# Attention scores as eight tiles of 32 rows by 64 keys, each over only the queries that its keys can meet

## The chip, the cores and the metric

The kernel runs on one core of a Trainium2 chip. The metric is device time in microseconds (us), the median of several executions.

## The reference, cut to what matters

Two independent problems of the same shape, A and B: 2048 positions, model width 1024, 32 heads of 32, and a sliding window of 256 keys.

```python
qkv = (x @ wqkv)                       # split into q, k, v; 32 heads, Dh = 32
scores = einsum("bhqd,bhkd->bhqk", q, k) * (Dh ** -0.5)
mask = (q_idx - k_idx >= 0) & (q_idx - k_idx < 256)
p = softmax(where(mask, scores, -1e9))
out = einsum("bhqk,bhkd->bhqd", p, v) @ wo
```

A block of 128 keys j thus meets the queries of blocks j (the lower triangle), j+1 (all) and j+2 (the upper triangle).

## The kernel before

Four heads form a group g. Its (key block, query block) pairs are handled in 180 *sessions* of four slots of 128 queries. Consecutive pairs with the same key block are one *run*; the sessions are mostly of runs of 3+1, 2+2 or 1+3 slots. A session issues the score matmuls, ScalarE takes the exponential of the whole buffer, GpSimd zeroes what the mask excludes, and some sessions later PV matmuls (p times v) use the result. In between, TensorE works on the projections.

```python
    def session(now):
        es = entries_of(now)
        n = len(es)
        st = ps_st.tile([P, 4, SLOTS, P], F32, name="st")     # four PSUM banks, one for each head
        ...
        while a < n:                                          # for each run a..b
            ...
            for r in range(4):                                # four heads = four 32-row tiles
                nc.tensor.matmul(
                    st[:, r, a:b, :],
                    lhsT=kT[32 * r:32 * r + 32, j * P:(j + 1) * P],
                    rhs=qT[32 * r:32 * r + 32, q * P:(q + b - a) * P],
                    start=True, stop=True, tile_position=(32 * r, 0))
            a = b
        pt = ptp.tile([P, 4, SLOTS, P], BF16, name="pt")
        nc.scalar.activation(out=pt[...], in_=st[...], func=ACT.Exp, bias=-SHIFT, scale=cfg.scale)
        # ... GpSimd masks of the first and third block of a run
```

Around PV, which uses four tiles of 128 rows by 32 columns, the projections are cut in the same way to avoid a change of array shape; ahead of a score session, where the shape does change, a median of 105 ns lies between the end of the streaming and the first score matmul. That takes four pairs of weight load and matmul where one would do:

```python
    def by_columns(out, lo, hi, lhsT, rhs, start, stop):
        if whole[0]:
            nc.tensor.matmul(out[:, lo:hi], lhsT=lhsT, rhs=rhs, ...)
            return
        for c in range(0, P, 32):
            nc.tensor.matmul(out[c:c + 32, lo:hi], lhsT=lhsT[:, c:c + 32], rhs=rhs, ...,
                             tile_position=(0, c))
```

## Time and profile before

| | before |
|---|---|
| time, median (lowest to highest) | 609.3 us (609.28 to 609.43, 3 runs) |
| span of the profiled execution | 607.6 us |
| TensorE on the chain that ended last | 96% |
| score matmuls (line L451), their share of the chain | 1488, 10% |
| TensorE instructions in the profile (matmuls and weight loads) | 25,624 |

In the profile, PE is TensorE's matmuls and PEld its weight loads. A group's line gives shapes and count, then busy time and mean duration, then the idle time before it and what ended that. A timeline line gives start, length, engine, source line, what is written and read, and in brackets the idle time before. A matmul's recorded length is not the time that it adds (one of 512 columns is recorded with 379 ns, and the next group of the same shape starts 216 ns after it), so the distance between starts says more than lengths do.

### The profile page before, as it was taken

The numbers are of one execution on the slowest core, as the hardware profiler recorded it, in microseconds if no ns is written. First come the engines' busy times: TensorE is split into PE (matmuls) and PEld (weight loads), VectorE is DVE, ScalarE is ACT, GpSimd is POOL, SyncE is SP. The second block draws the span as 40 slices with busy tenths as digits, with TensorE's granted clock in tenths as the row PEclk, the third lists the DMA queues.
The fourth block names the chain that finished last, engine by engine and source line by source line (L and its number), as shares of the span: only waits on it lengthen the run. The fifth ranks groups of instructions, "written<-read, shape, count | busy, mean of one in ns | idle before, by whom it ended". The sixth has DMA issues, their size and how long they took to land.

```text
span 607.6 us, 28768 instructions
## 1 busy us (share of the span) xinstructions
PE 593.6 (98%) x12786; PEld 344.3 (57%) x12838; DVE 468.4 (77%) x1199; ACT 441.1 (73%) x376; POOL 326.3 (54%) x630
## 2 busy tenths in 40 slices
PE   8999999999999999999999999999999999999996
PEld 6555466656655756564556756655455665545443
DVE  1677889898898898897888887898888887897200
ACT  3778887788888887877778877777776777785332
POOL 0565666665666666556555565555555655554000
PEclk9999999999999999999999999999999999999999
DMA  9833110111015501442111100112021040113222
GB/s 234 182 92 89 37 38 3 38 38 39 3 38 90 114 14 30 82 101 77 38 37 38 38 4 8 33 37 81 2 68 34 4 106 21 55 58 120 72 79 64
DMA packets 86802, 35.47 MB, mean 58 GB/s; under 512 B 65552, under 2 KB 86160, under 8 KB 86672
## 3 DMA queue, kind: packets, MB, share of 16 engines
q1 hardware_dynamic: 85632, 33.31, 22.2%
q8 instruction: 102, 1.67, 1.2%
q10 hardware_dynamic: 1040, 0.26, 0.2%
q14 instruction: 28, 0.23, 0.1%
HBM read 17.83 MB, written 8.39 MB: 43 GB/s over the span
## 4 chain that ended last, share of the span: by engine, by line
PE 96%; ACT 2%; issue 1%; DMA 1%; ACTq 0%
PE pp L176 44%; PE pp L172 28%; PE acc L513 13%; PE st L451 10%; ACT pt L459 1%; DMA oT<-in_A_x_dram 1%; PE acc L582 0%; PE pp L568 0%; ACT kT L190 0%; ACT vt L190 0%; PE st L582 0%; ACT osb L190 0%; PE pp L805 0%; ACTq L190 0%
## 5 line engine op out<-in xcount | busy, mean ns | idle before, releaser
L459 ACT ACTIVATE pt<-st 128x2048 bf16<-128x2048 f32 x180 | 338.0, 1878 | 91.6 <-PE st L451 73.5
L471 POOL TENSOR_SCALAR_AFFINE_SELECT pt<-pt 128x512 bf16<-128x512 bf16 x224 | 154.5, 690 | 145.7 <-ACT pt L459 143.1
L467 POOL TENSOR_SCALAR_AFFINE_SELECT pt<-pt 128x512 bf16<-128x512 bf16 x256 | 179.2, 701 | 85.8 <-ACT pt L459 85.8
L524 DVE RECIPROCAL rinv<-acc 128x128 f32<-128x128 f32 x128 | 122.0, 953 | 57.0 <-PE acc L513 56.4
L176 PE MATMUL pp<-xT,wqk 128*32 128x512 bf16 x2712 | 163.1, 379 | 0.0
L481 DVE TENSOR_TENSOR both<-pt 128x512 bf16<-128x512 bf16 x224 | 137.1, 651 | 0.0
L176 PEld LDWEIGHTS <-wqk 128*32 128x32 bf16 x2712 | 69.3, 97 | 54.2 <-issue 0.4
L172 PE MATMUL pp<-xT,wqk 128*128 128x512 bf16 (+1 forms) x323 | 76.7, 369 | 4.1 <-issue 2.4
L176 PE MATMUL pp<-wv,xT 128*32 128x256 bf16 x2436 | 75.9, 273 | 0.0
L451 PE MATMUL st<-qT,kT 32*128 32x384 bf16 (+2 forms) x1488 | 71.5, 269 | 0.1
L176 PEld LDWEIGHTS <-xT 128*32 128x32 bf16 x2436 | 63.8, 97 | 6.2
L529 DVE STREAM_SHUFFLE wide<-rinv 128x128 f32<-128x128 f32 x256 | 64.6, 298 | 0.0
L513 PE MATMUL acc<-pt,vt 128*32 128x128 bf16 (+1 forms) x2160 | 63.3, 239 | 0.0
L172 PE MATMUL pp<-wo_sb,oT 128*128 128x512 bf16 (+1 forms) x269 | 59.3, 373 | 1.3 <-issue 0.9
L451 PEld LDWEIGHTS <-kT 32*128 32x128 bf16 x1488 | 22.2, 92 | 64.5 <-issue 63.3
L190 ACT CAST osb<-pp 128x512 bf16<-128x512 f32 (+1 forms) x52 | 30.0, 577 | 39.1 <-PE pp L172 24.4
L531 DVE TENSOR_TENSOR oT<-acc,wide 128x256 bf16<-128x256 f32 x128 | 54.3, 425 | 4.4
L176 PE MATMUL pp<-wo_sb,oT 128*32 128x512 bf16 x952 | 55.6, 379 | 0.0
L172 PEld LDWEIGHTS <-wqk 128*128 128x128 bf16 x362 | 33.4, 98 | 37.0 <-issue 6.8
L172 PE MATMUL pp<-wv,xT 128*128 128x256 bf16 x415 | 50.9, 273 | 1.4 <-ACT kT L190 0.6
L513 PEld LDWEIGHTS <-vt 128*32 128x32 bf16 x2160 | 35.9, 96 | 26.4 <-issue 24.1
L172 PEld LDWEIGHTS <-xT 128*128 128x128 bf16 x415 | 38.9, 98 | 12.0 <-issue 6.1
(46 smaller groups left out, 386.5 us busy)
## 6 DMA issues: line engine op xcount, KB each, us to landing
out_dram<-osb SPq DMA_DIRECT2D x63, 128.0 KB, 1.8
wqk<-in_B_wqkv_dram SPq DMA_DIRECT2D x32, 128.0 KB, 2.5
wqk<-in_A_wqkv_dram SPq DMA_DIRECT2D x24, 128.0 KB, 2.7
wo_sb<-in_A_wo_dram SPq DMA_DIRECT2D x16, 128.0 KB, 2.2
wv<-in_B_wqkv_dram SPq DMA_DIRECT2D x16, 128.0 KB, 2.8
wo_sb<-in_B_wo_dram SPq DMA_DIRECT2D x16, 128.0 KB, 2.4
oT<-in_A_x_dram SPq DMA_DIRECT2D x4, 256.0 KB, 5.4
wv<-in_A_wqkv_dram SPq DMA_DIRECT2D x2, 512.0 KB, 5.9
```

What stands on the lines that cost most here:

```text
L172: nc.tensor.matmul(out[:, lo:hi], lhsT=lhsT, rhs=rhs, start=start, stop=stop, skip_group_check=True)
L176: nc.tensor.matmul(out[c:c + 32, lo:hi], lhsT=lhsT[:, c:c + 32], rhs=rhs, start=start, stop=stop, tile_position=(0, c), skip_group_check=True)
L190: nc.scalar.copy(out=out, in_=in_)
L451: nc.tensor.matmul(st[:, r, a:b, :], lhsT=kT[32 * r:32 * r + 32, j * P:(j + 1) * P], rhs=qT[32 * r:32 * r + 32, q * P:(q + b - a) * P], st ...
L459: nc.scalar.activation(out=pt[:, :, :n, :].rearrange("p r a q -> p r (a q)"), in_=st[:, :, :n, :].rearrange("p r a q -> p r (a q)"), func= ...
L467: nc.gpsimd.affine_select(out=blk, in_=blk, pattern=[[0, 4], [1, P]], compare_op=ALU.is_ge, fill=0.0, base=0, channel_multiplier=-1)
L471: nc.gpsimd.affine_select(out=blk, in_=blk, pattern=[[0, 4], [-1, P]], compare_op=ALU.is_gt, fill=0.0, base=0, channel_multiplier=1)
L481: nc.vector.tensor_tensor(out=both[:, :, h, :], in0=pts[s0][:, :, a0, :], in1=pts[s1][:, :, a1, :], op=ALU.add)
L513: nc.tensor.matmul(acc[32 * r:32 * r + 32, o:o + w_], lhsT=lhsT, rhs=src[:, r, :, :], start=(x == 0), stop=(x == len(moves) - 1), tile_pos ...
L524: nc.vector.reciprocal(out=rinv[:], in_=acc[:, 2 * P:3 * P])
L529: nc.vector.stream_shuffle(out=wide[:, h * P:(h + 1) * P], in_=rinv[:], mask=[16 * h] * 32)
L531: nc.vector.tensor_tensor(out=oTs[(pi, k)][:, t, (p % 2) * 256:(p % 2 + 1) * 256], in0=acc[:, 0:256], in1=wide[:], op=ALU.mult)
```

## The change

The intent: at either end of a run, a corner of 64 keys by 64 queries is always masked, so it need not be computed. The lower 64 keys of a block meet only the first 320 of a run's 384 queries, the upper 64 only the last 320. With tiles of 32 rows by 64 keys, each half streams only those. The buffer is kept for the whole program and zeroed once, so that the places no longer written hold finite numbers.

```diff
+HALF = 64
...
-        st = ps_st.tile([P, 4, SLOTS, P], F32, name="st")
+        st = scores
+        flat = st[:].rearrange("p r a q -> p r (a q)")
...
-            for r in range(4):
-                nc.tensor.matmul(
-                    st[:, r, a:b, :],
-                    lhsT=kT[32 * r:32 * r + 32, j * P:(j + 1) * P],
-                    rhs=qT[32 * r:32 * r + 32, q * P:(q + b - a) * P],
-                    start=True, stop=True, tile_position=(32 * r, 0))
+            for c in range(2):
+                lo = HALF if c == 1 and q == j else 0
+                hi = (b - a) * P - (HALF if c == 0 and q + b - a == j + 3 else 0)
+                keys = slice(j * P + c * HALF, j * P + (c + 1) * HALF)
+                for r in range(4):
+                    rows = slice(32 * r, 32 * r + 32)
+                    nc.tensor.matmul(
+                        flat[c * HALF:(c + 1) * HALF, r, a * P + lo:a * P + hi],
+                        lhsT=kT[rows, keys], rhs=qT[rows, q * P + lo:q * P + hi],
+                        start=True, stop=True, tile_position=(32 * r, c * HALF),
+                        skip_group_check=True)
             a = b
...
+    scores = ps_st.tile([P, 4, SLOTS, P], F32, name="st")
+    nc.vector.memset(scores[:, 1:4], 0.0)
...
-    flips.append(ps_st.tile([P, 4, SLOTS, P], F32, name="st")[:, 0].rearrange("p a q -> p (a q)"))
+    flips.append(scores[:, 0].rearrange("p a q -> p (a q)"))
...
+    nc.vector.memset(scores[:, 0:1], 0.0)
```

## The prediction

> **What bounds the kernel now.** I read the busy shares first, then the chain that ended last, then the groups by line and form, then the timeline around one score session, and last the start times of single matmuls in the trace. From the page:
>
> ```profile
> PE 593.6 (98%) x12786; PEld 344.3 (57%) x12838; DVE 468.4 (77%) x1199; ACT 441.1 (73%) x376; POOL 326.3 (54%) x630
> ...
> PE 96%; ACT 2%; issue 1%; DMA 1%; ACTq 0%
> PE pp L176 44%; PE pp L172 28%; PE acc L513 13%; PE st L451 10%; ACT pt L459 1%; DMA oT<-in_A_x_dram 1%; PE acc L582 0%; PE pp L568 0%; ACT kT L190 0%; ACT vt L190 0%; PE st L582 0%; ACT osb L190 0%; PE pp L805 0%; ACTq L190 0%
> ```
>
> TensorE is the chain for 96% of the span, and the score matmuls of L451 are 10% of it, some 61 us. The other engines have slack of 23% and more. The groups split by form:
>
> ```profile
> L451 PE MATMUL st<-qT,kT 32*128 32x384 bf16 x448 | 37.7, 326 | 0.1
> L451 PE MATMUL st<-qT,kT 32*128 32x128 bf16 x544 | 29.6, 219 | 0.0
> L451 PE MATMUL st<-qT,kT 32*128 32x256 bf16 x496 | 25.6, 273 | 0.0
> ```
>
> Four matmuls (one for each head, each in its own 32 rows) make a group: 112 groups of 384 columns, 136 of 128 and 124 of 256. The busy times can't be added up, because the durations overlap; the timeline is the better view of what a session of four slots costs:
>
> ```profile
> 302.36 0.60 PE L176 MATMUL pp<-xT,wqk 128*32 128x512 bf16 x8
> ...
> 302.89 0.12 PEld L451 LDWEIGHTS <-kT 32*128 32x128 bf16 x8 [0.42 <-issue]
> 302.90 0.40 PE L451 MATMUL st<-qT,kT 32*128 32x384 bf16 x8
> 303.22 0.29 PEld L513 LDWEIGHTS <-vt 128*32 128x32 bf16 x16 [0.21 <-issue]
> 303.23 0.51 PE L513 MATMUL acc<-pt,vt 128*32 128x128 bf16 x16
> 303.40 1.88 ACT L459 ACTIVATE pt<-st 128x2048 bf16<-128x2048 f32 x1 [0.75 <-ACT vt L190]
> ```
>
> The first row is two groups of four; within one array shape the trace starts the next group 216 ns after one of 512 columns, 109 ns after one of 256, 56 ns after one of 128: 0.418 ns a column plus 2.5 ns. So this projection has streamed its columns at 302.36 + 2x0.216 = 302.79 us. The scores start 0.11 us later although no operand is missing, and the PV matmuls start 0.33 us after the scores. Of that 0.33 the streaming of 384 + 128 columns is only 0.214.
>
> Taking the start times of all 180 sessions, the medians are 105 ns from the end of the streaming before to the first score matmul, and 328 ns from there to the next other matmul. In the session above the 384-column group took 174 ns up to the next group's start (160 streaming, 2.5 usual, some 11.5 more that only a first group after a change of shape shows), and the 128-column group 153 ns up to the first PV matmul (53 streaming, 100 for the change back). A session thus costs about 433 ns, 180 of them 78 us, and **only half of it, 213 ns, is columns streaming**. The rest is two changes of array shape.
>
> Is PE waiting for the exponential, which must have read the score buffer (there is just one)? The waits say the opposite:
>
> ```profile
> ACT pt L459 <- PE st L451: 73.5, 113, 1.3
> PEld L451 <- issue: 63.3, 177, 0.4
> ```
>
> ScalarE waits for the scores 113 times, and what precedes the score weight loads is "issue", not ScalarE. So time taken off or put on a score session goes straight to the end.
>
> [...] a 128-column load is read as four runs of 32 and takes 90 to 98 ns, no longer than a 32-column one (92 to 97). A 64-column load can then be the longest of the three; no run here shows it yet. [...] The trace shows tiles overlapping in one direction only at a time: four row tiles in the scores, and four column tiles in the PV and projection matmuls, start within 9 to 11 ns of each other. Rows and columns together occur nowhere in it.
>
> **The change part by part.**
>
> *Removed: columns.* A full run of three query blocks goes from 384 columns to 320 in each half of the keys: the lower 64 keys meet queries 0 to 319, the upper 64 meet 64 to 383. With 4 slots a session there are three main patterns, 56 sessions each, and 12 others. If the two halves truly overlap and each goes ahead independently:
> - runs 3+1: lower 320+128 = 448 columns, upper 320+64 = 384. The longer is 448 instead of 512.
> - runs 2+2: lower 192+256, upper 256+192: 448.
> - runs 1+3: lower 64+320, upper 128+320: 448.
> Eight of the other twelve keep 512, four go to 448. So 172 sessions lose 64 columns: 172 x 64 x 0.417 ns = **4.6 us**, the ceiling. It is under 1%.
>
> *Added: issue skew.* Score matmuls go from 1488 to 2976, weight loads likewise. The trace issues a pair of load and matmul each 3.4 ns or so. The upper half's four come after the lower half's four, so they start about 14 ns later. In the 2+2 and 1+3 patterns the upper half ends last, so all 14 ns lie at the end of the session; in 3+1 the lower half ends last, and the skew is hidden. Playing the order of issue through for all 180 sessions with these numbers leaves a gain of 27 ns for 3+1, 13 for the next two, mean 17: **3.1 us** in all.
>
> *Added: slower weight loads.* The 11.5 ns that a first group shows is about what 32 columns take (13 ns), so I read it as the exposed weight load. If a 64-column load is unsplit, 64 columns stand there instead: +13.5 ns a session, 180 x 13.5 = 2.4 us. Then **0.6 us** of gain remain. Later loads of the session are issued ahead while the first group streams and stay hidden. I take a point between 0.6 and 3.1, 2.0 us.
>
> *Unchanged:* both edges of 100 to 105 ns (the tiles are still not those of the neighbours), the exponential (still 128x2048, 1878 ns), the masks, PV, and the order in which everything is emitted, since the scheduler's constants are not touched.
>
> *The fills.* The buffer becomes permanent and is zeroed once, so that places never written hold finite numbers; the masks still remove them. A 256-column fill takes 0.27 us on VectorE in the trace, so the 1536-column fill is an estimated 1.6 us, and stands in 4.73 us of idle time before VectorE's first copy. The 512-column one is an estimated 0.55 us in the 1.30 us idle before its next work at 11.93 us, and the first scores only start at 13.83 us. Both cost nothing. I see no new wait from keeping the buffer: the first score matmul already waits for the previous exponential.
>
> Sum: 609.3 - 2.0 = **607.3 us**.
>
> **The rivals.**
> 1. *The two halves serialise.* If the tiles of one 32-row strip with different columns don't overlap, a session streams about 896 columns instead of 512: 384 x 0.417 = 160 ns more, 180 times, 28.8 us, 638 us. For it: no instruction of the kernel combines row and column tiles, and both halves write the same four PSUM banks. Against: PV's four column tiles write one bank and have different moving data, and still start within 10 ns[...]. I give it 10%.
> 2. *The halves overlap but advance in lockstep*, each group waiting for the longer of both. Then 2+2 keeps 256+256 = 512 and gains nothing but pays the skew; two thirds of the saving are left, minus the costs above: about 607.5 to 610. For it: in the trace all tiles of a group have the same number of columns. [...]
> 3. *The score buffer or ScalarE becomes the bound.* ScalarE is busy 73% and gets its scores no later than now; ends at the same time, 607 to 609.
> 4. *The edges change,* [...] Each 10 ns on one edge is 180 x 10 = 1.8 us either way. The trace shows such an effect already: the edge is 96 ns after 128x128 matmuls, 106 after four column tiles, which is the skew of the four.
>
> **Range and chances.** Over 2% faster would need 12.2 us, nearly three times the ceiling of streaming; only shorter edges could give it: 0.03. Over 2% slower needs 68 ns a session, so serialisation or something like it: 0.11. Within 2%: 0.86. For the range I take the ceiling and some edge gain below, 603.5, and edges or loads 10 to 20 ns worse than assumed above, 611.
>
> **What would show it.** The score line has 2976 matmuls with at most 320 columns. Right: eight start within about 28 ns, the 320-column group starts its successor some 147 to 161 ns after itself instead of 174, and the score session goes from 328 ns to 311 to 325, with the edge before it still at 105. The first-group excess reads 11 or 25 ns and settles the weight load. Wrong: the upper half starts only when the lower half has streamed (rival 1), or a 2+2 session stays at 328 or more (rival 2), or PE now shows waits on ScalarE. The prediction fails if PE's other lines change their spacing, for instance through the larger number of instructions.

## The result, and the profile after

| | before | after |
|---|---|---|
| time, median (lowest to highest), 6 runs each | 609.37 us (609.18 to 610.27) | 610.9 us (610.07 to 612.45) |
| ratio | | 1.0026 (95%: 1.0008 to 1.0043) |
| span of the profiled execution | 607.6 us | 608.4 us |
| score matmuls | 1488 | 2976 |

A ratio is the mean time of one kernel's runs over that of the other's of the same rounds, so it is not quite the ratio of the medians. Executions over 1.5% slower than the fastest of the same kernel are left out of the means. The change makes the kernel a little slower, by a quarter of a per cent.

From the page of the changed kernel, busy shares and the chain that ended last:

```profile
PE 593.7 (98%) x14274; PEld 351.9 (58%) x14326; DVE 470.7 (77%) x1201; ACT 441.1 (73%) x376; POOL 326.2 (54%) x630
...
PE 96%; ACT 2%; issue 1%; DVE 0%; ACTq 0%
PE pp L177 44%; PE pp L173 28%; PE acc L520 14%; PE st L458 10%; ACT pt L466 1%; PE pp L577 1%; PE acc L591 0%; ACT kT L191 0%; ACT vt L191 0%; PE st L591 0%; ACT osb L191 0%; DVE top L126 0%; PE pp L815 0%; DVE ones L791 0%; ACTq L191 0%
```

At this resolution nothing has moved: the scores (now L458) are still 10% of the chain. By form the columns are trimmed as intended, and the weight loads got slower, 103 ns where those of before had 92 (first line: before; the others: after):

```profile
L451 PEld LDWEIGHTS <-kT 32*128 32x128 bf16 x1488 | 22.2, 92 | 64.5 <-issue 63.3 <-DVE top L184 0.8 <-ACT kT L190 0.4
```

```profile
L458 PE MATMUL st<-qT,kT 32*64 32x320 bf16 x896 | 38.6, 307 | 0.3
L458 PE MATMUL st<-qT,kT 32*64 32x128 bf16 x560 | 30.3, 226 | 0.0
L458 PEld LDWEIGHTS <-kT 32*64 32x64 bf16 x2976 | 29.1, 103 | 65.0 <-issue 64.0 <-DVE top L185 0.8
```

**Where the time went.** I compared the two traces from each score session's start to the next. For each pattern of session the median difference is taken as the session's own (for the twelve rare sessions, the difference in the sessions themselves); what an interval has above that is something else. Between the two traces of before this account leaves 0.02 us, so it can be trusted to a few hundredths. This gives, in the profiled executions:

| | us |
|---|---|
| first score session starts (loads at the start) | -0.46 |
| the 180 sessions themselves | -1.00 |
| five intervals in which TensorE stood still | +1.51 |
| nine intervals with some 44 ns more each | +0.40 |
| the rest, up to the start of the last session | -0.04 |
| after the start of the last session | +0.35 |
| sum: span 607.62 to 608.37 | +0.76 |

The profiled execution is a fast one of the changed kernel (610.1 us, median 610.9), so the table accounts for about half of the 1.5 us between the medians. The first row is scatter (the second execution of the changed kernel had +0.70). The sessions did save 1.0 us: 3+1 sessions, from the first score matmul to the next other weight load, went from 325 to 312 ns, 2+2 and 1+3 stayed (326), and the edge ahead of all of them became 2 ns shorter. The two rows that took more than that away are shown next.

**The stops.** This is the timeline of the weight loads near one of them in the changed kernel:

```profile
209.21 0.11 PEld L177 LDWEIGHTS <-xT 128*32 128x32 bf16 x4
209.53 0.14 PEld L458 LDWEIGHTS <-kT 32*64 32x64 bf16 x11 [0.21 <-issue]
210.00 0.11 PEld L458 LDWEIGHTS <-kT 32*64 32x64 bf16 x5 [0.33 <-issue]
210.26 0.22 PEld L173 LDWEIGHTS <-xT 128*128 128x128 bf16 x3
```

and the same session in the kernel before:

```profile
209.78 0.12 PEld L451 LDWEIGHTS <-kT 32*128 32x128 bf16 x8 [0.21 <-issue]
210.11 0.99 PEld L172 LDWEIGHTS <-xT 128*128 128x128 bf16 x10 [0.21 <-issue]
```

In the middle of sixteen like loads, all from the same finished kT, nothing starts for 0.41 us, and the profile gives the reason as "issue": no semaphore event, from which it infers who released whom, and no other engine. The matmuls stop with them: one session's, with the gap in the changed kernel (0.80 us) and without it in the one before (0.40 us):

```profile
209.53 0.80 PE L458 MATMUL st<-qT,kT 32*64 32x64 bf16 x16
```

```profile
209.78 0.40 PE L451 MATMUL st<-qT,kT 32*128 32x128 bf16 x8
```

Seven such gaps over 120 ns are in this trace (28.56, 78.67, 210.00, 249.14, 344.63, 381.60 and 486.33 us; that at 249 shows no excess in the account above, that at 345 some 0.05 us, the other five are its five intervals). Counting TensorE's instructions in program order, its sequencer's included, **all seven stand at the same place modulo 256**. I call each stretch of 256 TensorE instructions from one such place to the next a block, and the place its edge. The trace has a queue q8 of the kind "instruction", with packets of 16,384 bytes. Their number is about one for each 256 of TensorE's instructions (102 packets for 25,624 matmuls and weight loads before, 100.1 times 256; 114 for 28,600 after, 111.7 times 256), so I take them for TensorE's (first before, then after; packets, MB, share):

```profile
q8 instruction: 102, 1.67, 1.2%
```

```profile
q8 instruction: 114, 1.87, 1.3%
```

Each of the seven gaps ended 1.24 to 1.59 us after the last such packet had landed. My reading, from these traces alone: a packet brings a block's instructions, and at these places TensorE gets to the next block before it can be used. Two things in the traces fit that. Pairing packets and block edges in order, a packet starts a median of 0.5 us after the edge before in the changed kernel; for the stop at 210.00 us it started 0.81 us after that edge, took 1.00 to land, and TensorE went on 1.45 later, 3.26 us in all, where the block's own instructions needed 2.84. And of 1,333 edges in the twelve traces of this text none was passed sooner than 1.09 us after the landing of its packet; in the two traces of before none sooner than 1.67.

**The waits on ScalarE.** The kernel before, around one session:

```profile
397.11 0.40 PE L451 MATMUL st<-qT,kT 32*128 32x384 bf16 x8
...
397.60 1.88 ACT L459 ACTIVATE pt<-st 128x2048 bf16<-128x2048 f32 x1 [1.20 <-PE st L451]
...
399.38 0.58 ACT L190 CAST qT<-pp 128x512 bf16<-128x512 f32 x1
...
400.01 0.10 PEld L176 LDWEIGHTS <-wqk 128*32 128x32 bf16 x3 [0.19 <-issue]
```

and the changed kernel:

```profile
397.11 0.38 PE L458 MATMUL st<-qT,kT 32*64 32x320 bf16 x16
...
397.64 1.88 ACT L466 ACTIVATE pt<-st 128x2048 bf16<-128x2048 f32 x1 [1.23 <-PE st L458]
...
399.42 0.58 ACT L191 CAST qT<-pp 128x512 bf16<-128x512 f32 x1
...
400.05 0.10 PEld L177 LDWEIGHTS <-wqk 128*32 128x32 bf16 x3 [0.23 <-issue]
```

The scores start at the same time and TensorE gets through them sooner, yet the exponential starts 0.04 us later, so the copy behind it on ScalarE is 0.04 us later, and TensorE, which needs the projection bank that this copy frees, too. In all 3+1 sessions the exponential now starts a median of 529 ns after the first score matmul instead of 498, in 2+2 470 instead of 449, in 1+3 449 as before. (The profile has the semaphore of the last score matmul of a 3+1 session at a median of 457 ns after the first one's start instead of 426.) Only a few sessions have no slack for it. Seven of the nine intervals end at a projection matmul that waits for a copy of ScalarE, an eighth at one that waits for a copy of VectorE. The ninth, at 344.6 us, is no such wait: it is the gap at the block edge at 344.63.

**The fills** cost nothing, as their lines in the groups by form and VectorE's idle time around them show (1.34 and 0.49 us; the first scores at 13.37 us):

```profile
L572 DVE MEMSET st<- 128x1536 f32 x1 | 1.3, 1338 | 0.3 <-issue 0.3
L609 DVE MEMSET st<- 128x512 f32 x1 | 0.5, 485 | 0.1
```

### The profile page after: what moved, and what is told of

Read it like the earlier page. It is cut to its first block, busy times and chain, and to the rows that moved or that the text cites. A ratio compares the mean times of both kernels' runs of the same rounds, so it can differ in the third digit from the quotient of the medians.

```text
span 608.4 us, 31747 instructions
## 1 busy us (share of the span) xinstructions
PE 593.7 (98%) x14274; PEld 351.9 (58%) x14326; DVE 470.7 (77%) x1201; ACT 441.1 (73%) x376; POOL 326.2 (54%) x630
## 4 chain that ended last, share of the span: by engine, by line
PE 96%; ACT 2%; issue 1%; DVE 0%; ACTq 0%
PE pp L177 44%; PE pp L173 28%; PE acc L520 14%; PE st L458 10%; ACT pt L466 1%; PE pp L577 1%; PE acc L591 0%; ACT kT L191 0%; ACT vt L191 0%; PE st L591 0%; ACT osb L191 0%; DVE top L126 0%; PE pp L815 0%; DVE ones L791 0%; ACTq L191 0%
## 5 line engine op out<-in xcount | busy, mean ns | idle before, releaser
L458 PE MATMUL st<-qT,kT 32*64 32x320 bf16 (+4 forms) x2976 | 71.3, 259 | 0.3
L458 PEld LDWEIGHTS <-kT 32*64 32x64 bf16 x2976 | 29.1, 103 | 65.0 <-issue 64.0
```

Of the source, the lines that this page charges most:

```text
L458: nc.tensor.matmul(flat[c * HALF:(c + 1) * HALF, r, a * P + lo:a * P + hi], lhsT=kT[rows, keys], rhs=qT[rows, q * P + lo:q * P + hi], star ...
```

## The experiments

The theory to be tested, called F in the expectations: the trimming saves a little, and the added instructions make TensorE run out of instructions at the edges of blocks of 256, which costs more. The first expectations speak of 0.6 us saved and 1.45 us of stops; that was from a rougher account, which had put part of the stops into the sessions, and the table above (1.00 and 1.51) replaces it. All outputs of all runs were correct. The counts of gaps below are of gaps over 120 ns at a block's edge with a packet landing 1.05 to 1.7 us before their end; a few tenths of a microsecond in each sum would be there without a stop (a change of array shape, 103 to 105 ns ahead of a score session, may fall in one).

### The changed kernel once more

No edit.

> The changed kernel once more, for its spread and for a second trace. Theory F (starved front end): the score sessions save 0.6 us, but five times TensorE stood still for 0.14 to 0.41 us with no wait on anything, each time where its instruction stream enters another block of 256, and these 1.45 us together are the loss. Then this trace again shows a few such stops, all at the same place of a block, not necessarily in the same blocks, and the time is 609.8 to 612.5 us, more scattered than before's. Rival S (start and end): the loss is the new fills or the end of the program; then the trace shows a later first score session or a later end, and no stops. Rival N (noise): ratio to before within 0.1% of 1.

Measured: 611.33 us (610.89 to 612.37), 1.0027 (1.0014 to 1.004) of the kernel before. The trace has five gaps at block edges, 2.2 us in all, at 29.93, 111.09, 211.99, 251.18 and 383.76 us. Three of these are the instructions at which the first trace stopped at 28.56, 210.00 and 381.60 us, now for 587, 850 and 347 ns instead of 375, 411 and 124. By the same account as above its sessions save 1.00 us, the stops cost 2.11 and the waits on copies (eight) 0.35. At one of the three the stop is longer where the packet came later: for 411 ns at 210.00 us the packet started 0.81 us after the edge before, for 850 ns at 211.99 us 1.23 us after. That this makes the kernel's larger scatter fits, but isn't shown. The start lay 0.70 us late here and 0.46 early in the first trace: rival S gets no support.

### The kernel before once more

No edit.

> The kernel before once more, for a second trace. Theory F (the front end starves where 256 TensorE instructions run in less than about 3.2 us): no stop of 60 ns or more that the first trace of before lacks, since its fastest block took 3.2 us there and got by; the first score session within 0.7 us of the first trace's, which is the scatter of the loads at the start. Rival: stops come by chance with any kernel; then this trace has some too.

Measured: 609.4 us. Against the first trace of before no interval between sessions differs by more than 25 ns, and neither of the two traces has a gap at a block edge.

### As many instructions, but the old tiles

```diff
 # on the kernel before
-            for r in range(4):
-                nc.tensor.matmul(st[:, r, a:b, :], lhsT=kT[...], rhs=qT[32*r:32*r+32, q*P:(q+b-a)*P], ...)
+            w = (b - a) * P // PARTS                  # PARTS = 2
+            for c in range(PARTS):
+                for r in range(4):
+                    nc.tensor.matmul(flat[:, r, a*P + c*w:a*P + (c+1)*w], lhsT=kT[...],
+                                     rhs=qT[32*r:32*r+32, q*P + c*w:q*P + (c+1)*w], ...)
```

> The kernel before, with each score matmul of four row tiles cut into two halves of its queries: as many TensorE instructions as the changed kernel, but neither 64-key tiles nor fewer columns, nor a kept buffer. Theory F: the score sessions alone give +5 ns each (2.5 ns for each further group), +0.9 us; beyond that the stops appear here too, at block edges, for 0.5 to 3 us more: 610.8 to 613 us. Rival T (the 32 by 64 tiles cause the stops): no stops, 610.2 to 610.5 us.

Measured: 612.74 us (612.08 to 614.67), ratio 1.0057 (1.0043 to 1.0071). Sessions went from 325 to 330 ns, +0.91 us in all as expected. The trace has five gaps at block edges, 1.7 us. One of them, at the same place in the program as the one shown above:

```profile
210.85 0.14 PEld L454 LDWEIGHTS <-kT 32*128 32x128 bf16 x11 [0.21 <-issue]
211.39 0.11 PEld L454 LDWEIGHTS <-kT 32*128 32x128 bf16 x5 [0.39 <-issue]
```

Eleven loads, a stop, five loads, exactly as with the 64-key tiles. So the stops need neither the new tiles nor the trimmed columns nor the kept buffer; **the number of instructions brings them**. Rival T falls. The intervals of 44 ns did not come here. They do not belong to the 64-key tiles, though: the next run has six of 40 ns with the old tiles. What they follow is how late the exponential of a 3+1 session starts, 498 ns after the first score matmul in the kernel before, 511 here, 529 in the changed kernel, 584 in the next run.

### Three times as many added

```diff
-PARTS = 2
+PARTS = 4
```

> The kernel before with each score matmul cut into four quarters of its queries: 4464 score matmuls more than before, three times what the change adds, same array shape. Sessions +15 ns each by the 2.5 ns for every further group, +2.8 us. Theory F: blocks of 256 go by still faster, so stops get more and longer, at least twice the 1.6 us of the cut in two: 615 us or more. Rival (the stops have to do with tiles of 64 columns or with chance): 612 to 613 us.

Measured: 632.64 us (631.47 to 634.34), ratio 1.0386 (1.037 to 1.0402). 36 gaps at block edges, 14.9 us. The view of waits now has whole lines for TensorE waiting for nothing but its own issue, where the kernel before, once the first microseconds are over, has only "PE pp L172" with 3.5 us in 22 pieces, none longer than 0.2:

```profile
PE pp L177 <- issue: 2.8, 5, 1.3
PE st L454 <- issue: 2.1, 4, 0.8
PE acc L516 <- issue: 0.8, 2, 0.4
```

The columns are total us, times, longest us. The direction was expected, the size not: three times the added instructions gave nearly nine times the stops. Part of the time is not stops: 2+2 sessions took 341 ns as worked out, but 3+1 and 1+3 sessions took 369 and 378, by their medians some 56 x (28 + 37) ns = 3.6 us more than expected. These have pieces of 32 columns, and the trace shows where the time is: groups of four such matmuls start 25 ns apart, where 32 columns and the usual 2.5 ns would be 16. Nine ns at each of three or four groups are the 28 and 37. Why they come no closer isn't shown.

### What the trimmed columns are worth

```diff
 # on the changed kernel
-                lo = HALF if c == 1 and q == j else 0
-                hi = (b - a) * P - (HALF if c == 0 and q + b - a == j + 3 else 0)
+                lo = 0
+                hi = (b - a) * P
```

> The changed kernel with all columns kept: eight tiles of 32 by 64, each over all queries of the run. What the fewer columns are worth: by the spacing in the trace 26 to 31 ns a session, so a session of some 352 ns instead of 325 and +5.5 us over the changed kernel less what the stops change: 614 to 617 us. A rival in which column tiles share the read of their queries or in which the halves advance in lockstep would leave 2+2 sessions as long as in the changed kernel (326 ns).

Measured: 616.59 us (615.07 to 616.91), ratio 1.0105. Sessions of every main pattern take 352 or 353 ns: 27 ns more than the 2+2 and 1+3 sessions of the changed kernel, 40 more than its 3+1 sessions. So the trimmed columns are worth what streaming says, 64 x 0.417 = 27 ns, and splitting a session into 64-key tiles without trimming costs 27 (353 against 325 or 326 before). The two nearly cancel.

### The order of the halves

```diff
+        cols = [...]                      # columns of each half in this session
+        upper = cols[1] > cols[0]
...
-            for c in range(2):
+            for c in ((1, 0) if upper and a == 0 else (0, 1)):
```

> The changed kernel with the upper half first in the first run of the sessions in which the upper half is the longer chain (the 1+3 pattern). If the 14 ns of issue skew at the end of a session are real, the 1+3 sessions go from 326 to 313 ns, 56 x 13 = 0.7 us less than the changed kernel, with the stops unchanged in kind: 609 to 611.5 us. If the skew is no cost, sessions stay at 326.

Measured: 610.95 us (610.33 to 612.44), ratio 1.0022. The 1+3 sessions fell from 326 to 312 or 313 ns, as expected, so the issue skew is real and is avoidable there. Over all sessions the saving against before rose from 1.00 to 1.73 us, the 0.7 us expected. The kernel's time did not follow clearly (0.4 us under the changed kernel of the same rounds, with overlapping ranges): this trace has six gaps at block edges, 2.7 us. An inconclusive run for the total, a clear one for the session.

### Sixteen tiles of 32 by 32

```diff
-HALF = 64
+HALF = 32
...
-            for c in range(2):
-                lo = HALF if c == 1 and q == j else 0
-                hi = (b - a) * P - (HALF if c == 0 and q + b - a == j + 3 else 0)
+            for c in range(4):
+                lo = c * HALF if q == j else 0
+                hi = (b - a) * P - ((3 - c) * HALF if q + b - a == j + 3 else 0)
```

> Sixteen tiles of 32 rows by 32 keys, each over the queries that its 32 keys can meet (288 columns of a full run instead of 320). Theory on the weight load: the excess of the first group falls from 24.5 ns (64 columns) back to about 11.5 (32 columns)[...]; the skew grows to 40 ns, 12 pairs of 3.4. Together the sessions come to some 313 ns, 2.3 us less than before. Theory F then loses all of that and more to the stops, since it adds 8928 instructions: 611 to 616 us. If the excess stays at 24.5 ns, the reason isn't the number of columns loaded.

Measured: 631.8 us (628.71 to 633.49), ratio 1.0372; 36 gaps at block edges, 16.5 us. What a first group takes above its streaming until its tiles start the second group is 12.7 ns in the kernel before (loads of 128 columns), 26.7 in the changed one (64), and 13.3 here (32). It goes with the runs of columns that the trace records as a load's source: four runs of 32 for each of the 1488 score loads before, one run of 64 for each of the 2976 in the changed kernel. My reading, an estimate from the 0.417 ns a column of the same traces, is that one run stands exposed once a session: 13.3 ns for 32 columns, 26.7 for 64. It isn't shown that what is exposed is the load. Up to the next weight load the sessions took 286, 326 and 326 ns, a mean of 313 as worked out. But what counts is the next matmul, and in 3+1 sessions it comes 32 ns after its weight load here, where 2 ns are usual. Up to the next matmul they took 318, 329 and 328 ns, where the kernel before has 327, 329 and 327 and the one with the better order 314, 330 and 314. So of the 2.3 us expected of the sessions only some 0.4 came, and **the sixteen tiles' sessions are not the best ones**. Why that matmul comes late isn't shown.

### Only where it gains

The new tiles only in sessions in which the longer half has fewer columns than before and the halves differ; the four old matmuls in the others.

```diff
 # on the kernel with the better order
+            if cols[0] == cols[1] or max(cols) == SLOTS * P:
+                for r in range(4):
+                    ...                        # the old matmul of 128 keys, into the kept buffer
+                a = b
+                continue
```

> Candidate: 64-key tiles only in the sessions that gain by them (3+1, and 1+3 with the upper half first in the first run), the four old 128-key matmuls in the 2+2 sessions and the others that gain nothing. Sessions save 1.5 us against before; 944 score matmuls are added instead of 1488, so fewer stops, though most of the fast blocks still have some added: 0.5 to 1.5 us of stops. 608.3 to 609.8 us, within 0.2% of before either way, and 1 to 2.5 us under the changed kernel.

Measured: 609.57 us (608.87 to 610.41), ratio 0.9997 (0.9983 to 1.001): the same as before. Sessions saved 1.76 us. Fewer stops came, three, but one took 1.46 us:

```profile
487.66 0.38 PE L470 MATMUL st<-qT,kT 32*64 32x128 bf16 x15
489.20 0.29 PE L470 MATMUL st<-qT,kT 32*64 32x320 bf16 x1 [1.17 <-issue]
```

Fifteen matmuls, a stop, and the sixteenth: its packet had started at 486.80 and landed at 487.72 us, 1.49 before the stop ended. The lag is within the 1.24 to 1.59 us of the first trace of the changed kernel; the packet came late.

### Only where it gains and the blocks are slow enough

From the start times of the first trace of before I worked out how long each block of 256 would take for any choice of sessions. Before's fastest takes 3.18 us and has no stop. In the changed kernel the blocks that ended in the stops at 78.67, 210.00, 381.60 and 486.33 us took 3.03, 2.84, 3.10 and 2.97. (The one at 28.56 is of another kind: its block took 5.8 us, but its packet started late, 3.9 us after the edge before, among the large loads of the start.) The line is not sharp: the block of the changed kernel that ended at 378.26 us took 2.97 us, too, and had no stop. Leaving nine more sessions as they were keeps nearly all blocks at 3.18 us or more.

```diff
+PLAIN = {26, 32, 38, 44, 48, 50, 56, 59, 68}
...
-            if cols[0] == cols[1] or max(cols) == SLOTS * P:
+            if cols[0] == cols[1] or max(cols) == SLOTS * P or now in PLAIN:
```

> The mixed kernel, but with the old four matmuls kept in nine more sessions, chosen so that, by the start times of the first trace of before, no block of 256 TensorE instructions is run through faster than the fastest one of before (3.18 us; the mixed kernel has some of 2.9 and 3.0). 107 sessions with 64-key tiles, 13 ns each: 1.4 us; eight waits of 43 ns on ScalarE stay: 0.35 us. Theory F: no stop above 100 ns, and 608.1 to 608.9 us, under the kernel before by 0.1 to 0.2% and under the mixed one by 1 us. Rival (stops come with 64-key tiles wherever they stand): about as many as in the mixed kernel, 609.3 us or more.

Measured: 608.87 us (608.38 to 609.37), ratio 0.9984 (0.997 to 0.9998) of the kernel before. It is the only version here whose interval lies wholly under 1, if barely. Sessions saved 1.73 us against before. One stop of 362 ns was left, at 49.97 us, where none was expected: its block took 3.2 us without the stop, but its packet started 1.2 us after the edge before; the intervals of 44 ns came six times. TensorE's share of the chain is up a point:

```profile
PE 97%; ACT 2%; issue 0%; DVE 0%; ACTq 0%
PE pp L178 44%; PE pp L174 29%; PE acc L533 14%; PE st L471 5%; PE st L459 4%; ACT pt L479 1%; PE pp L590 1%; PE acc L604 0%; ACT kT L192 0%; ACT vt L192 0%; PE st L604 0%; ACT osb L192 0%; DVE top L127 0%; PE pp L828 0%; DVE ones L804 0%
```

It still has 872 more score matmuls than before, only 72 fewer than the version above, yet all of that one's stops but one are gone, the long one at 489 us with them. This is the other direction of the proof, from one trace of each: taking instructions out of the fast blocks takes stops away.

### All instructions moved within their blocks

```diff
 # on the changed kernel
-    keep_warm(6)
+    for n in range(6 * 8):
+        nc.tensor.matmul(warm[:, n % 8 * 64:(n % 8 + 1) * 64], lhsT=blank[:, 0:P],
+                         rhs=blank[:, 0:64], start=True, stop=True, skip_group_check=True)
```

> The changed kernel with 84 more TensorE instructions ahead of everything (the six warm-up matmuls of 512 columns cut into 48 of 64, the same columns), so that every later instruction stands elsewhere in its block of 256. Theory F: the stops leave their places (near 28.5, 210, 382 and 486 us in the program) or change their size by 0.1 us and more, and others come, each again where a block of 256 begins; the time may be anywhere between 609.5 and 613 us. Rival (stops belong to places of the program, such as loads that are busy there): they stay where they were with the same length.

Measured: 611.74 us (611.3 to 612.12), ratio 1.003. The stops at 210 and 382 us are gone; the longest are now at 348.57 and 490.69 us (912 and 672 ns), and there is one of 180 ns at 477.86, all three at the same place modulo 256 as ever, 1.31 to 1.51 us after a packet landed. The stop of 1.0 us near 30.5 us in this trace is no stop of this kind: the profile gives a late load of x as its end. So a stop belongs to a place in a block, not to a place in the program.

### The stops in one table

| kernel | score matmuls | gaps at block edges | their sum, us | time, us |
|---|---|---|---|---|
| before, two traces | 1488 | 0 and 0 | 0 | 609.4 to 609.8 |
| only where it gains, slow blocks | 2360 | 1 | 0.4 | 608.87 |
| only where it gains | 2432 | 3 | 2.3 | 609.57 |
| changed, two traces | 2976 | 7 and 5 | 1.8 and 2.2 | 610.9 and 611.33 |
| changed, moved by 84 | 2976 | 5 | 2.2 | 611.74 |
| changed, other order | 2976 | 6 | 2.7 | 610.95 |
| changed, all columns | 2976 | 3 | 1.7 | 616.59 |
| before, cut in two | 2976 | 5 | 1.7 | 612.74 |
| before, cut in four | 5952 | 36 | 14.9 | 632.64 |
| sixteen tiles | 5952 | 36 | 16.5 | 631.8 |

## Why the prediction was right or wrong

"Within 2%" (0.86) was right, and 610.9 us lies in the range, but at its very edge; the second set of runs, 611.33, lies outside. That it lies inside is luck: the upper end was set for edges or loads 10 to 20 ns worse than assumed, which did not come, and the stops, which had no price, used up that room. The point, 607.3, had the wrong sign: -2.0 forecast, +1.5 measured. Step by step:

- **Removed columns: right.** 27 ns a session, by the run with all columns kept.
- **Issue skew: right.** The last matmul of the first group starts 23 ns after the first, instead of 10, and the other order of halves took 13 ns off the 1+3 sessions.
- **Slower weight loads: right in kind, and the choice of a point was wrong.** I named 0.6 us as what is left if a 64-column load is exposed in full, and then took 2.0, between that and 3.1. The excess of the first group rose as for full exposure (26.7 against 12.7 ns). The sessions saved 1.0 us, some 0.4 of it through the 2 ns at the edges. So 1.0 of the 3.6 us by which the point is off comes from here.
- **Unchanged edges, fills: right.** The edge ahead of a session is a median of 103 ns instead of 105, nearly unchanged, and both fills lie in idle time.
- **"I see no new wait", and that ScalarE gets its scores no later: wrong.** Eight waits of 44 ns on copies, seven of them ScalarE's, 0.35 us. That the exponential starts later although TensorE is through sooner is measured; why is open.
- **The term that was missing: the number of instructions, and the stops at block edges that came with it.** The prediction has it only as its last clause, "for instance through the larger number of instructions", without a price. It cost 1.5 us in the first trace and 2.1 in the second, and turned a small gain into a small loss. This is shown: the old tiles with as many instructions have the stops, four times as many score matmuls have 15 us of them, and taking instructions out of the fast blocks left one.
- **Rivals.** Serialising (1) fell: in a 2+2 session the upper four start 14 ns after the lower four. Lockstep (2) fell: of the second group the lower half starts at 107 ns and the upper at 147, each when its own tile is through. Rival 3 is true in a small way (the waits on ScalarE's copies). Rival 4 came to 2 ns.

Some 0.35 us between the two profiled executions lies after the start of the last score session and isn't explained. It isn't in the engines' work: the last copy of the output ends 48.87 us after that start before and 48.86 after, so the difference comes behind it, where the last stores and the end of the program are. The second trace of before has 0.10 more than the first, the ten traces of the other kernels have 0.15 to 0.67, so it is hardly scatter alone.

## What to carry to other kernels

On a TensorE that is busy nearly all the time (98% of the span here), price a change by instructions as well as by columns: find how long the kernel takes for 256 TensorE instructions where it is fastest. The fastest block of before, 3.18 us, had no stop, and four blocks of the changed kernel that ended in one had needed 2.84 to 3.10 us, though another of 2.97 had none; there the stops cost 1.5 us and the sessions saved 1.0. The sign was a gap in front of both loads and matmuls that the profile ends with "issue", at the same place modulo 256; those counted here took from 0.12 us, the limit of the count, to over 1 us (1.46 in the mixed kernel). The 64-key tiles paid where the chain of the longer half shrank (3+1 sessions, 325 to 312 ns); where it didn't (2+2 sessions, 326 ns before and after), leave the large tile.
